# Moving the sums of the second weights between VectorE and GpSimd in a fused attention and feed-forward kernel

## The chip, the cores and the metric

One core of a Trainium2 chip. The time is that of one execution on the device in microseconds, the median of several runs; lower is better.

## What is computed

Attention within chunks of 64 rows, over 8 heads of 64 features, and then a layer norm with a gain `g`, a feed-forward net of 512 to 2048 to 512 features with a ReLU between, and a sum with its input. There are 8 x 576 = 4608 rows, and all data are float32 (the arrays arrive as given below; the kernel's weights are handed over as 64-bit words).

```
def _attn_ref(q, k, v):                       # 8, 8, 576, 64; chunks of 64 rows
    scores = scale * q_c @ k_c.transpose(0, 1, 2, 4, 3)
    scores = scores - max(scores); attn = exp(scores)
    attn = attn / (sum(attn) + 1e-09)
    return attn @ v_c
def _moe_ref(x, g_ln, w_ch1, w_ch2):          # x: 8, 576, 512
    xn = (x - mu) / sqrt(var + 1e-06) * g_ln
    return x + max(xn @ w_ch1, 0.0) @ w_ch2
```

## The kernel before

**Tiles and units.** The rows form 18 pairs of 256 rows, and two pairs make a tile. The first three tiles go through the net in the plain way. The other six make two units of two pairs of pairs each, whose products are done by a scheme with seven products in place of eight (Strassen's in Winograd's form). For that the weights are needed as seven sums and differences of their blocks. Each float32 product is made of three passes: a rounded high part and the rest, called `hh` and `hl` (or `his` and what is left) in the code.

**The sums of the weights.** `prepare` (stream S, on GpSimd) makes those of the first weights during the second tile and the start of the third, and writes them to `wa` in DRAM. `mix` makes those of the second weights during the third tile: for each of eight parts p (weights 2p and 2p + 1), two sums of the high and the low half (L975, 128x512), four sums and differences of blocks (L982, 128x256), a rounded copy by ScalarE (L985), two subtractions that give the rest (L988, 128x512), and the writes to `wb` in DRAM (L992, L993). Each part does that in eight steps. Streams a, b, c are parts 1, 2, 3 on VectorE; T is parts 4 and 5 on GpSimd, V part 6 on GpSimd, W part 7 on VectorE; d is part 0, read back from DRAM, on VectorE.

**The order by hand.** All engines work off their own queues in the order in which the program issues to them. That order is written down: `THIRD` gives, for each of 32 tokens of the third tile's net, which streams take one step each before the token. A token `u1` is a first product of the net (twelve matmuls, L560) and its split into `hh` (ScalarE, L573) and `hl` (VectorE, L574); a token `u` is a second product (twelve matmuls, L584). C, G, D and H are the attentions of the pairs of the first unit: G1 loads q and k, G2 is the scores (L304), G3 their maxima (VectorE, L311), G4 the difference (VectorE, L336), G5 the exponent (ScalarE), G6 to G9 the transposes by VectorE (L375), G10 the sums, G11 the product with v (L404), G12 its scaling. D9 is a scaling (L430), D10 the statistics (L448 to L454, the last of them `rstd` on GpSimd), D11 the centring (VectorE, L460), D12 the scaling by `rstd` (ScalarE), D13 and D14 the transposes by TensorE (L492) and their copies. P and Q (`combine`) make the first unit's operands from the rows: casts on ScalarE (L781), differences on VectorE (L788), subtractions on GpSimd (L785).

**Places.** PSUM has two banks named `s` (one buffer, for scores, transposes and some products), two named `h` (for the first products, and for G11, which takes both) and four named `y`. A tile of SBUF with the tag `w5`, say, takes the place of weight 5 when that is no longer read. A new tile in a place waits for all readers of the old one.

**The units.** `unit_ffn` runs the seven products (L1031), four groups of fourteen, with sums on VectorE into `hu` (L1040) and copies on ScalarE into `snap` (L1037), and then the second products (L943). Weights come through a ring of six places of 512 KB. `weave` lets other streams take steps at given costs, where each product of six matmuls costs 6.

Of the kernel before, what the change touches and what calls it, by code (L numbers as in the profile page):

```python
# [8 lines left out]
F32 = mybir.dt.float32  # L9
# [32 lines left out]
    23: "BCS", 24: "BCS", 25: "CS", 26: "S", 27: "CCS", 28: "CS", 29: "CCS", 30: "CDS", 31: "CDDS", 32: "DS",  # L42
}
THIRD = {
    0: "CS", 1: "CS", 2: "DDGS", 3: "DS", 4: "DDS", 5: "DS", 6: "DGSaa", 7: "GGHSTTaa", 8: "DGTTabb", 9: "Daaabb",
    10: "GGPTcc", 11: "HGGPTTbcc", 12: "GTTTbb", 13: "GTTbc", 14: "GGHPcc", 15: "GHPTc", 16: "GHPTT", 17: "GPTVV",
    18: "HHGPVV", 19: "HGP", 20: "HGPV", 21: "HHPVVd", 22: "HPV", 23: "WW", 24: "HWW", 25: "Hdd", 26: "QQWdd",
    27: "QRWW", 28: "QWd", 29: "QXXNdd", 30: "QQRd", 31: "Q",
}
ROOMS = {1: (3, 9), 2: (6,)}  # L50

# [4 lines left out]
AT_END = (0, 6, 11, 18, 33, 37, 40, 48, 54, 82, 92, 97, 104, 109, 121, 133, 146)  # L56
PAIR_STEPS = (STEPS, BY_TENSOR, WIDE, AT_END)
HALVES = ((512, 8), (612, 10))
REST = (2, 6, 20)


# [41 lines left out]
def chunk_attention_ffn(ctx: ExitStack, tc: tile.TileContext, qkv, v01, g, w, out):  # L103
# [31 lines left out]
    def weights(f):  # L135
        if f not in wp:
            wp[f] = const.tile([P, 2, NW], F32R, name="wp", tag=f"w{f}")
        return wp[f][:, 0, :], wp[f][:, 1, :]
# [514 lines left out]
    def bring(pairs):  # L653
        for pair in pairs:
            back[pair] = unspill(pair)
            yield
# [312 lines left out]
                    yield 3.17  # L969
                    self.advance(t + (k + 1) / 2)  # L970

    def mix(p, t_, his, parts_of, engine):
        for k in range(2):
            high, low = parts_of(k)
            engine.tensor_tensor(out=t_[:, k], in0=high, in1=low, op=ALU.add)  # L975
            yield
        b11, b12, b21, b22 = (t_[:, k // 2, k % 2 * PAIR : (k % 2 + 1) * PAIR] for k in range(4))
        for k, (out, x, y, op) in enumerate((
            (b11, b12, b11, ALU.subtract), (b12, b22, b12, ALU.subtract), (b22, b11, b22, ALU.subtract),
            (b21, b21, b22, ALU.add),  # L980
        )):
            engine.tensor_tensor(out=out, in0=x, in1=y, op=op)  # L982
            if k % 2:
                yield
        nc.scalar.copy(his, t_)  # L985
        yield
        for k in range(2):
            engine.tensor_tensor(  # L988
                out=t_[:, k].bitcast(F32R), in0=t_[:, k], in1=his[:, k].bitcast(F32), op=ALU.subtract
            )  # L990
            yield
        nc.sync.dma_start(wb[:, p, 0], his.rearrange("p f (a n) -> p (f a) n", a=2).bitcast(F32))  # L992
        nc.sync.dma_start(wb[:, p, 1], t_.rearrange("p f (a n) -> p (f a) n", a=2))  # L993
        yield

    def mix_early(pool, tag, ps, engine):
        for p in ps:
            t_ = pool.tile([P, 2, 2, DM], F32, name="mixed", tag=tag)
            yield from mix(
                p, t_[:, 0], t_[:, 1].bitcast(F32R),  # L1000
                lambda k: [x[:, DM:].bitcast(F32) for x in weights(2 * p + k)], engine,
            )

    def mix_again(tag, p):
        t_ = const.tile([P, 2, 2, DM], F32, name="mixed", tag=tag)
        for k in range(2):
            nc.sync.dma_start(t_[:, :, k], w2d[2 * p + k])
        yield
        yield from mix(
            p, t_[:, 0], t_[:, 1].bitcast(F32R), lambda k: [t_[:, 0, k], t_[:, 1, k]], nc.vector  # L1010
        )

    def unit_ffn(u):
        first = 2 * LEAD + 4 * u
        hu = {}
        for n in range(2):
            for f in range(NF):
                if f // 2 not in hu:
                    hu[f // 2] = shared.setdefault(
                        f"h{f // 2}", None  # L1020
                    ) or const.tile([P, 2, 2, DM], F32, name="hu", tag=f"w{8 + f // 2}")
                    shared[f"h{f // 2}"] = hu[f // 2]
        snaps = [raws.tile([P, n, DM], F32, name="snap", tag=g) for n, g in ((4, "raw"), (2, "wf"))]
        snaps = [x[:, i] for x in snaps for i in range(x.shape[1])]

# [39 lines left out]
        for q in range(NF // 4):  # L1065
            banks = [ps_y.tile([P, DM], F32, name="y") for _ in range(4)]
            c_, a_ = banks[0::2], banks[1::2]
            h = [hu[2 * q], hu[2 * q + 1]]
            s = [snaps[:3], snaps[3:]]

            def pair_of():
                w = ring.take()[:, : 2 * DM].rearrange("p (i h n) -> p i h n", i=2, h=2)
                return w[:, 0], w[:, 1]

            steps = []
            for e in range(2):
                steps += [
                    (c_, e, "2", None),
                    (a_, e, "1", lambda e: (copy(s[e][0], a_[e]), add(h[e][:, 0, 0], c_[e], s[e][0]))),
                ]  # L1080
            for e in range(2):
                steps += [
                    (a_, e, "6", lambda e: copy(s[e][1], a_[e])),
                    (c_, e, "5", lambda e: copy(s[e][2], c_[e])),
                ]
            for e in range(2):
                steps += [
                    (a_, e, "7", lambda e: add(h[e][:, 1, 1], a_[e], s[e][2])),
                    (c_, e, "3", lambda e: add(h[e][:, 1, 0], c_[e], s[e][1])),
                ]  # L1090
            for e in range(2):
                steps += [
                    (a_, e, "4", lambda e: nc.scalar.activation(h[e][:, 0, 1], a_[e], AF.Relu))
                ]
            for i, (bank, e, name, then) in enumerate(steps):
                if i % 2 == 0:
                    w01 = pair_of()
                product(bank[e], w01[i % 2], name, name in "215")
                yield 6
                if i % 2:  # L1100
                    ring.fetch()
                if then:
                    then(e)
                if name == "7":
                    waiting.append((14 * q + i + 2, h[e][:, 1, 1]))
                if waiting and waiting[0][0] <= 14 * q + i:
                    relu(waiting.pop(0)[1])
                if q > 0 and i in (4, 6):
                    mix_1(2 * (q - 1) + i // 2 - 2)
                if q == NF // 4 - 1:  # L1110
                    plan.advance((i + 1 - len(steps)) * 0.945)
                    if i in (12, 13):
                        mix_1(2 * q + i - 12)
# [48 lines left out]
    with tc.manual_schedule():  # L1162
        nc.scalar.activation(minus, ident, AF.Copy, scale=-1.0)
        play(START, now)
        now.update(
            A=now.pop("E"), B=tiles[2].attention(1), C=tiles[3].attention(0, True), D=tiles[4].attention(0, True),
            G=tiles[3].attention(1), H=tiles[4].attention(1, True, pt_raw=True), S=prepare(), R=start_ring(), T=mix_early(raws, "raw", (4, 5), nc.gpsimd),
            V=mix_early(const, "w7", (6,), nc.gpsimd), W=mix_early(const, "w8", (7,), nc.vector), X=bring(range(2 * LEAD - 2, 2 * LEAD)),
            a=mix_early(const, "w1", (1,), nc.vector), b=mix_early(const, "w2", (2,), nc.vector), c=mix_early(const, "w3", (3,), nc.vector),
            d=mix_again("w9", 0), P=combine(0, 0), Q=combine(0, 1),  # L1170
        )
        now.update(zip("u1", tiles[1].ffn(0, 2, room=ROOMS[1])))
        play(layout(ROOMS[1], SECOND), now)
        streams = {}

        def following(u, n):
            n, u = n % 4, u + n // 4
            if (u, n) not in streams and u < UNITS:
                by_pe = len(PAIR_STEPS[n]) == len(BY_TENSOR)
                streams[u, n] = tiles[LEAD + 2 * u + n % 2].attention(n // 2, pt_by_pe=by_pe)  # L1180
            return streams.get((u, n), iter(" "))

        now["N"] = following(1, 0)
        now.update(zip("u1", tiles[2].ffn(0, 2, room=ROOMS[2])))
        play(layout(ROOMS[2], THIRD, True), now)
        side = [(at, now["Q"]) for at in REST]
        for u in range(UNITS):
            if u + 1 < UNITS:
                for n in range(4):
                    begin, steps = BEGINS[n], PAIR_STEPS[n]  # L1190
                    side += [(begin + at, following(u + 1, n)) for at in steps]
                    side.append((begin + steps[0], following(u + 1, n + 1)))
                for half, (begin, step) in enumerate(HALVES):
                    stream = combine(u + 1, half)
                    side += [(begin + i * step, stream) for i in range(13)]
            side = weave(unit_ffn(u), side)
        assert not side
# [35 lines left out]
```

## Time and profile before

| | us |
|---|---|
| median of 3 runs | 839.59 (837.94 to 843.39) |
| the profiled execution | 839.96 |
| its span, first to last instruction | 838.0 |
| TensorE busy | 818.5 (98%) |
| VectorE busy | 643.5 (77%) |
| ScalarE busy | 345.8 (41%) |
| GpSimd busy | 179.3 (21%) |

The third tile's net runs from about 228 to 338 us of the span. A row of the timeline gives the start, the busy time, the engine, the line, the operation, what it writes and reads, its size and count, and in brackets the engine's idle time before it with what ended it. PE is TensorE, DVE VectorE, ACT ScalarE, POOL GpSimd; a q behind a name means the engine's queue. A row of stretches gives the limits, the length, the busy time and count of PE, PEld (weight loads), DVE, ACT and POOL, and then the granted TensorE clock, the share of the DMA engines and GB/s.

### The profile page before, as it was taken

To read this page: it belongs to the slowest core of one execution; us is meant where nothing else is said; L and a number is where in the kernel's file an instruction comes from. 1 tells how busy PE (TensorE), PEld (TensorE's weight loads), DVE (VectorE), ACT (ScalarE), POOL (GpSimd) and SP (SyncE) were. 2 spreads that over 40 slices of the span, in tenths; PEclk is the share of its full clock that TensorE was granted. 3 is DMA by queue.
4 is the path that set the end of the run, shared out by engine and by line. 5 is a ranking of instruction groups with operands and counts; after the bars stand their busy time and mean duration, and the time that the engine had idled before them with its cause. 6 is when DMAs were issued, how large, how long until landed. Compare 5 with 4: busy or idle time off the path is not lost.

```text
span 838.0 us, 16961 instructions
## 1 busy us (share of the span) xinstructions
PE 818.5 (98%) x6746; PEld 713.6 (85%) x6746; DVE 643.5 (77%) x1023; ACT 345.8 (41%) x545; POOL 179.3 (21%) x148
## 2 busy tenths in 40 slices
PE   7999999999998799999999999999999999999998
PEld 4888888888887587888899998788999988889998
DVE  6989966777659998779788998898889953248854
ACT  4776431122333234243364453434555632255432
POOL 0111006463855374100000270000002700000000
PEclk9999999999999799999999999999999999999999
DMA  9998417948884435978889659788796686668662
GB/s 357 334 267 237 157 45 240 327 163 289 306 287 160 192 126 214 398 258 265 286 251 305 212 177 352 236 275 253 226 303 218 182 295 190 190 198 278 212 214 101
DMA packets 117278, 200.62 MB, mean 239 GB/s; under 512 B 8784, under 2 KB 75856, under 8 KB 115280
## 3 DMA queue, kind: packets, MB, share of 16 engines
q1 hardware_dynamic: 115904, 194.82, 68.7%
q0 software_dynamic: 1296, 4.72, 2.9%
q8 instruction: 53, 0.87, 0.4%
q14 instruction: 25, 0.20, 0.1%
HBM read 141.84 MB, written 48.76 MB: 227 GB/s over the span
## 4 chain that ended last, share of the span: by engine, by line
PE 89%; DVE 7%; DMA 2%; ACT 1%; issue 1%; SPq 0%; DVEq 0%; ACTq 0%
PE y L943 29%; PE y L1031 26%; PE y L584 14%; PE h L560 14%; PE s L304 2%; DVE pt_sb L375 2%; PE h L404 1%; DVE mixed L982 1%; DMA wp<-wfs 1%; DMA k_t<-qkv 1%; PE s L404 1%; PE s L330 0%; PE s L363 0%; PE s L353 0%; DVE mixed L975 0%
## 5 line engine op out<-in xcount | busy, mean ns | idle before, releaser
L1031 PE MATMUL y<-xc,ring 128*128 128x512 f32 x1008 | 235.2, 392 | 0.2 <-DVE hu L1040 0.2
L1031 PEld LDWEIGHTS y<-xc,ring 128*128 128x128 f32 x1008 | 187.5, 188 | 39.8 <-DVE hu L1040 0.6
L943 PE MATMUL y<-ring,hx 128*128 128x256 f32 x1272 | 158.0, 283 | 0.0
L943 PEld LDWEIGHTS y<-ring,hx 128*128 128x128 f32 x1272 | 155.0, 192 | 0.0
L560 PE MATMUL h<-xth,wp 128*128 128x512 f32 (+1 forms) x432 | 129.5, 370 | 0.9 <-DMA wp<-wfs 0.9
L1040 DVE TENSOR_TENSOR hu<-y,snap 128x512 f32<-128x512 f32 x72 | 49.2, 686 | 69.0 <-PE y L1031 34.7
L584 PE MATMUL y<-wp,hh 128*128 128x512 f32 x376 | 97.9, 399 | 0.0
L880 ACT ACTIVATE hx<-hu 128x512 fp32r<-128x512 f32 x106 | 65.8, 630 | 65.8 <-PE y L943 60.9
L560 PEld LDWEIGHTS h<-xth,wp 128*128 128x128 f32 x432 | 78.2, 188 | 15.4 <-DMA wp<-wfs 1.1
L785 POOL TENSOR_TENSOR xc<-rows,xc 128x512 fp32r<-128x512 f32 x28 | 60.5, 2173 | 128.8 <-ACT xc L781 127.2
L584 PEld LDWEIGHTS y<-wp,hh 128*128 128x128 f32 x376 | 70.1, 191 | 14.3
L889 DVE TENSOR_TENSOR hx<-hu,hx 128x512 fp32r<-128x512 f32 x90 | 67.4, 758 | 15.1 <-ACT hx L880 13.2
L560 PE MATMUL h<-xtl,wp 128*128 128x512 f32 (+1 forms) x216 | 78.3, 367 | 0.0
L573 ACT ACTIVATE hh<-h 128x512 fp32r<-128x512 f32 (+1 forms) x53 | 28.5, 545 | 109.0 <-PE h L560 109.0
L1037 ACT COPY snap<-y 128x512 f32<-128x512 f32 x72 | 41.7, 585 | 73.4 <-PE y L1031 73.4
L943 PE MATMUL y<-ring,hh 128*128 128x256 f32 x496 | 71.8, 283 | 0.0
L574 DVE SCALAR_TENSOR_TENSOR hl<-h,hh 128x512 fp32r<-128x512 f32 (+1 forms) x53 | 32.9, 627 | 45.8 <-ACT hh L573 45.4
L943 PEld LDWEIGHTS y<-ring,hh 128*128 128x128 f32 x496 | 65.2, 192 | 0.2
L584 PE MATMUL y<-wp,hl 128*128 128x512 f32 x188 | 51.9, 390 | 0.0
L880 ACT ACTIVATE hh<-hu 128x512 fp32r<-128x512 f32 x62 | 38.8, 631 | 31.6 <-PE y L943 29.1
L375 DVE STREAM_TRANSPOSE pt_sb<-p_sb 32x256 f32<-32x256 f32 x112 | 48.8, 436 | 3.6 <-ACT p_sb L339 1.7
L454 POOL TENSOR_TENSOR rstd<-vare,mhalf 128x2 f32<-128x2 f32 x12 | 10.0, 831 | 190.2 <-DVE vare L453 190.2
(146 smaller groups left out, 1084.4 us busy)
## 6 DMA issues: line engine op xcount, KB each, us to landing
ring<-wa SPq DMA_DIRECT2D x84, 512.0 KB, 4.6
ring<-wb SPq DMA_DIRECT2D x48, 512.0 KB, 3.8
ring<-w2d SPq DMA_DIRECT2D x36, 512.0 KB, 3.8
raw<-w SPq DMA_DIRECT2D x15, 1024.0 KB, 7.7
out<-x SPq DMA_DIRECT2D x22, 512.0 KB, 5.4
q_t<-qkv SPq DMA_DIRECT2D x17, 512.0 KB, 6.1
k_t<-qkv SPq DMA_DIRECT2D x17, 512.0 KB, 7.0
v_t<-qkv SPq DMA_DIRECT2D x32, 256.0 KB, 7.1
```

The lines of the kernel that those rows point to most:

```text
L375: nc.vector.transpose(out=pt_sb[quad(2 * h2 + j), :, c, quad(i)], in_=p_sb[quad(2 * c + i), :, h2, quad(j)])
L560: nc.tensor.matmul(h, lhsT=(wh, wh, wl)[m][:, ks], rhs=(xth, xtl, xth)[m][:, k, :], start=i == 0, stop=i == len(terms) - 1,)
L573: nc.scalar.activation(hh, h, AF.Relu)
L574: nc.vector.scalar_tensor_tensor(out=hl, in0=h, scalar=0.0, in1=hh.bitcast(F32), op0=ALU.max, op1=ALU.subtract)
L584: nc.tensor.matmul(sums(pairs[j // 2])[j % 2], lhsT=(hh, hh, hl)[m], rhs=(wh, wl, wh)[m], start=f == 0 and m == 0, stop=f == NF - 1 and m ...
L785: engine.tensor_tensor(out=o[:, 1], in0=x, in1=o[:, 0].bitcast(F32), op=ALU.subtract)
L880: nc.scalar.activation(hh, self.split[i][2], AF.Relu if x == "1" else AF.Copy)
L889: nc.vector.tensor_tensor(out=hl, in0=x, in1=hh.bitcast(F32), op=ALU.subtract)
L943: nc.tensor.matmul(bank[j // 2][:, j % 2 * PAIR : (j % 2 + 1) * PAIR], lhsT=(hh, hh, hl)[m][:, j * P : (j + 1) * P], rhs=loaded[t // 2][:, ...
L1031: nc.tensor.matmul(bank, lhsT=w[:, (0, 0, 1)[m], ks], rhs=x[:, (0, 1, 0)[m], k, :], start=start and k == m == 0, stop=k == 1 and m == 2, s ...
L1037: nc.scalar.copy(out, bank)
L1040: nc.vector.tensor_tensor(out=out, in0=bank, in1=s, op=ALU.add)
```

## The change

Part 2 (stream b) goes from VectorE to GpSimd. Part 7 leaves the third tile: a stream of its own on GpSimd makes it in the first unit, at the costs `MIX_STEPS`, in the place of weight 13. Part 5 has a stream of its own (U), beside T for part 4. Parts 1, 2, 3 are put into the places of weights 0, 1, 2 and not 1, 2, 3, and part 1 begins at token 4 and not 6, part 2 at token 6 and not 8, part 3 at token 9 and not 10. Within several tokens the steps of a, c and d now come ahead of the attention's steps. `mix` makes the rounded copy in two halves and writes `wb` in four pieces of 256 KB and not two of 512 KB. The places of `hu` are handed out group by group.

```
 THIRD = {
-    0: "CS", 1: "CS", 2: "DDGS", 3: "DS", 4: "DDS", 5: "DS", 6: "DGSaa", 7: "GGHSTTaa", 8: "DGTTabb", 9: "Daaabb",
-    10: "GGPTcc", 11: "HGGPTTbcc", 12: "GTTTbb", 13: "GTTbc", 14: "GGHPcc", 15: "GHPTc", 16: "GHPTT", 17: "GPTVV",
-    18: "HHGPVV", 19: "HGP", 20: "HGPV", 21: "HHPVVd", 22: "HPV", 23: "WW", 24: "HWW", 25: "Hdd", 26: "QQWdd",
-    27: "QRWW", 28: "QWd", 29: "QXXNdd", 30: "QQRd", 31: "Q",
+    0: "CS", 1: "CS", 2: "DDGS", 3: "DS", 4: "aaDDS", 5: "aaDS", 6: "aDGSbb", 7: "aaGGHSbbTT", 8: "aDGTT", 9: "ccDb",
+    10: "ccGGPbbbT", 11: "HGGTT", 12: "cGTUU", 13: "GPUU", 14: "GGHP", 15: "ccGHPU", 16: "cGHPUU", 17: "GPUVV",
+    18: "HHGPVV", 19: "HGP", 20: "HGPV", 21: "HHPVVd", 22: "HPV", 24: "H", 25: "ddH", 26: "ddQQ", 27: "QR", 28: "dQ",
+    29: "ddQXXN", 30: "dQQR", 31: "Q",
 }
+MIX_STEPS = (24, 26, 30, 34, 54, 60, 62, 76)

-    def mix(p, t_, his, parts_of, engine):
+    def mix(p, engine, pool, tag, again=False):
+        both = pool.tile([P, 2, 2, DM], F32, name="mixed", tag=tag)
+        t_, his = ([both[:, i, k] for k in range(2)] for i in range(2))
...
-        nc.scalar.copy(his, t_)
-        yield
         for k in range(2):
-            engine.tensor_tensor(
-                out=t_[:, k].bitcast(F32R), in0=t_[:, k], in1=his[:, k].bitcast(F32), op=ALU.subtract
-            )
-            yield
-        nc.sync.dma_start(wb[:, p, 0], his.rearrange("p f (a n) -> p (f a) n", a=2).bitcast(F32))
-        nc.sync.dma_start(wb[:, p, 1], t_.rearrange("p f (a n) -> p (f a) n", a=2))
-        yield
+            nc.scalar.copy(his[k].bitcast(F32R), t_[k])
+        yield
+        for k in range(2):
+            engine.tensor_tensor(out=t_[k].bitcast(F32R), in0=t_[k], in1=his[k], op=ALU.subtract)
+            yield
+        for k in range(2):
+            for h, x in enumerate((his, t_)):
+                nc.sync.dma_start(wb[:, p, h, 2 * k : 2 * k + 2], x[k].rearrange("p (a n) -> p a n", a=2))
+        yield
...
+            for p in (2 * q, 2 * q + 1):
+                name = f"h{p}"
+                if name not in shared:
+                    shared[name] = const.tile([P, 2, 2, DM], F32, name="hu", tag=f"w{8 + p}")
+                hu[p] = shared[name]
...
-            G=tiles[3].attention(1), H=tiles[4].attention(1, True, pt_raw=True), S=prepare(), R=start_ring(), T=mix_early(raws, "raw", (4, 5), nc.gpsimd),
-            V=mix_early(const, "w7", (6,), nc.gpsimd), W=mix_early(const, "w8", (7,), nc.vector), X=bring(range(2 * LEAD - 2, 2 * LEAD)),
-            a=mix_early(const, "w1", (1,), nc.vector), b=mix_early(const, "w2", (2,), nc.vector), c=mix_early(const, "w3", (3,), nc.vector),
-            d=mix_again("w9", 0), P=combine(0, 0), Q=combine(0, 1),
+            G=tiles[3].attention(1), H=tiles[4].attention(1, True, pt_raw=True), S=prepare(), R=start_ring(), T=mix(4, nc.gpsimd, raws, "raw"),
+            U=mix(5, nc.gpsimd, raws, "raw"), V=mix(6, nc.gpsimd, const, "w7"), a=mix(1, nc.vector, const, "w0"),
+            b=mix(2, nc.gpsimd, const, "w1"), c=mix(3, nc.vector, const, "w2"), d=mix(0, nc.vector, const, "w9", True),
+            X=bring(range(2 * LEAD - 2, 2 * LEAD)), P=combine(0, 0), Q=combine(0, 1),
...
         side = [(at, now["Q"]) for at in REST]
+        stream = mix(NF // 2 - 1, nc.gpsimd, const, "w13")
+        side += [(at, stream) for at in MIX_STEPS]
```

More of the change, by code (lines that the diff above doesn't have):

```diff
@@ L970, in products @@
                     self.advance(t + (k + 1) / 2)
-    def mix(p, t_, his, parts_of, engine):
+    def mix(p, engine, pool, tag, again=False):
+        both = pool.tile([P, 2, 2, DM], F32, name="mixed", tag=tag)
+        t_, his = ([both[:, i, k] for k in range(2)] for i in range(2))
+        if again:
+            blocks = [[t_[k], his[k]] for k in range(2)]
+            for k in range(2):
+                nc.sync.dma_start(both[:, :, k], w2d[2 * p + k])
+            yield
+        else:
+            blocks = [[x[:, DM:].bitcast(F32) for x in weights(2 * p + k)] for k in range(2)]
         for k in range(2):
-            high, low = parts_of(k)
-            engine.tensor_tensor(out=t_[:, k], in0=high, in1=low, op=ALU.add)
+            engine.tensor_tensor(out=t_[k], in0=blocks[k][0], in1=blocks[k][1], op=ALU.add)
             yield
-        b11, b12, b21, b22 = (t_[:, k // 2, k % 2 * PAIR : (k % 2 + 1) * PAIR] for k in range(4))
+        b11, b12, b21, b22 = (t_[k // 2][:, k % 2 * PAIR : (k % 2 + 1) * PAIR] for k in range(4))
         for k, (out, x, y, op) in enumerate((
@@ L984, in mix @@
                 yield
-        nc.scalar.copy(his, t_)
+        for k in range(2):
+            nc.scalar.copy(his[k].bitcast(F32R), t_[k])
         yield
         for k in range(2):
-            engine.tensor_tensor(
-                out=t_[:, k].bitcast(F32R), in0=t_[:, k], in1=his[:, k].bitcast(F32), op=ALU.subtract
-            )
+            engine.tensor_tensor(out=t_[k].bitcast(F32R), in0=t_[k], in1=his[k], op=ALU.subtract)
             yield
-        nc.sync.dma_start(wb[:, p, 0], his.rearrange("p f (a n) -> p (f a) n", a=2).bitcast(F32))
-        nc.sync.dma_start(wb[:, p, 1], t_.rearrange("p f (a n) -> p (f a) n", a=2))
+        for k in range(2):
+            for h, x in enumerate((his, t_)):
+                nc.sync.dma_start(wb[:, p, h, 2 * k : 2 * k + 2], x[k].rearrange("p (a n) -> p a n", a=2))
         yield
[L996 to L1007, printed above, removed]
-        yield
-        yield from mix(
-            p, t_[:, 0], t_[:, 1].bitcast(F32R), lambda k: [t_[:, 0, k], t_[:, 1, k]], nc.vector
-        )
     def unit_ffn(u):
@@ L1015, in unit_ffn @@
         hu = {}
[L1016 to L1022, printed above, removed]
         snaps = [raws.tile([P, n, DM], F32, name="snap", tag=g) for n, g in ((4, "raw"), (2, "wf"))]
```

## The prediction

> **What bounds the kernel now.** I read the engine totals first, then the chain of waits in order of time, then the timelines of TensorE, VectorE and GpSimd where that chain leaves TensorE.
>
> ```profile
> PE 818.5 (98%) x6746; PEld 713.6 (85%) x6746; DVE 643.5 (77%) x1023; ACT 345.8 (41%) x545; POOL 179.3 (21%) x148
> ```
>
> TensorE is busy for 818.5 of 838.0 us, so little can be won: only where it stands still, or runs slowly, inside the third tile. These are its rows there.
>
> ```profile
> 253.85 0.60 PE L492 MATMUL s<-ident,xg 128*128 128x128 f32 x4
> ...
> 260.27 1.98 PE L584 MATMUL y<-wp,hh 128*128 128x512 f32 x8
> ...
> 269.85 0.33 PE L404 MATMUL h<-v_t,pt_sb 64*64 64x64 f32 x4
> 278.30 1.97 PE L404 MATMUL h<-v_t,pt_sb 64*64 64x64 f32 x60 [8.12 <-DVE hl L574]
> ...
> 333.04 1.22 PE L584 MATMUL y<-wp,last 128*128 128x512 f32 x3 [0.70 <-ACT last L573]
> ```
>
> The products of G's attention (L404) get through four matmuls and then stand for 8.12 us, until VectorE's `hl` frees the second `h` bank. At the tile's end 0.70 us are lost to ScalarE. The chain after the first stop, and the granted clock around it:
>
> ```profile
> 280.27 4.65 PE y L584 x12
> 284.92 5.45 PE h L560 x24
> 290.38 2.72 PE y L584 x12
> 274.00:278.00 4.00, 0.00 (x0) 0.00 (x0) 3.92 (x4) 0.32 (x1) 3.92 (x4) 0.50 0.09 37
> 278.00:282.00 4.00, 3.70 (x64) 3.27 (x65) 3.93 (x8) 0.72 (x1) 1.69 (x3) 0.50 0.00 0
> 282.00:286.00 4.00, 4.00 (x15) 3.15 (x14) 3.86 (x8) 0.00 (x0) 0.70 (x1) 0.76 0.96 336
> ```
>
> TensorE comes back at half clock (0.50; in these rows it is the third figure from the right): twelve matmuls of L584 take 4.65 us and not 2.72, a loss of 1.93, and of the 1.97 us of sixty L404 half is lost, so the clock costs 1.93 + 0.98 = 2.9 us. All that the third tile can give back is 8.12 + 2.9 + 0.70 = 11.7 us, 1.4%. Why VectorE is late stands in its own rows:
>
> ```profile
> 246.14 1.41 DVE L460 SCALAR_TENSOR_TENSOR xg<-x,mv,g_sb 128x512 f32<-128x512 f32 x2
> 247.91 0.69 DVE L574 SCALAR_TENSOR_TENSOR hl<-h,hh 128x512 fp32r<-128x512 f32 x1 [0.36 <-ACT hh L573]
> 248.52 2.44 DVE L975 TENSOR_TENSOR mixed<-wp 128x512 f32<-128x512 f32 x2
> 250.88 1.21 DVE L311 TENSOR_REDUCE top<-s 128x16 f32<-128x1024 f32 x1
> 252.12 1.22 DVE L336 TENSOR_TENSOR p_sb<-s,top 128x1024 f32<-128x1024 f32 x1
> 253.27 1.79 DVE L982 TENSOR_TENSOR mixed<-mixed 128x256 f32<-128x256 f32 x4
> 254.98 0.68 DVE L574 SCALAR_TENSOR_TENSOR hl<-h,hh 128x512 fp32r<-128x512 f32 x1
> 255.58 1.28 DVE L975 TENSOR_TENSOR mixed<-wp 128x512 f32<-128x512 f32 x2
> 257.11 1.29 DVE L988 TENSOR_TENSOR mixed<-mixed 128x512 fp32r<-128x512 f32 x2 [0.25 <-ACT mixed L985]
> 258.32 4.16 DVE L982 TENSOR_TENSOR mixed<-mixed 128x256 f32<-128x256 f32 x4
> 262.40 0.68 DVE L574 SCALAR_TENSOR_TENSOR hl<-h,hh 128x512 fp32r<-128x512 f32 x1
> 263.00 3.58 DVE L375 STREAM_TRANSPOSE pt_sb<-p_sb 32x256 f32<-32x256 f32 x8
> 266.61 3.30 DVE L975 TENSOR_TENSOR mixed<-wp 128x512 f32<-128x512 f32 x2
> 269.93 3.60 DVE L375 STREAM_TRANSPOSE pt_sb<-p_sb 32x256 f32<-32x256 f32 x8
> 273.56 4.09 DVE L982 TENSOR_TENSOR mixed<-mixed 128x256 f32<-128x256 f32 x4
> 277.57 0.68 DVE L574 SCALAR_TENSOR_TENSOR hl<-h,hh 128x512 fp32r<-128x512 f32 x1
> 246.31 1.13 POOL L454 TENSOR_TENSOR rstd<-vare,mhalf 128x2 f32<-128x2 f32 x1 [6.81 <-DVE vare L453]
> 247.42 2.38 POOL L692 TENSOR_TENSOR parts<-sums,parts 128x1024 fp32r<-128x1024 f32 x1
> 258.43 2.88 POOL L975 TENSOR_TENSOR mixed<-wp 128x512 f32<-128x512 f32 x2 [8.63 <-DMA wa<-parts]
> ```
>
> VectorE never rests from 248 to 278 us. The same operation has two prices: two sums of L975 take 1.28 us with GpSimd idle and 2.44 while GpSimd's L692 runs; four steps of L982 take 1.79 alone and 4.16 beside GpSimd's L975. Operations that read PSUM (L311, L336, L574) and the transposes keep their time. So two-input operations of VectorE on SBUF wait for a GpSimd operation to end. The Trainium skill, "SBUF — State Buffer", section "SBUF: two separate sides", calls this an exclusive lock between the two engines, held for a whole instruction. By it, work moved to GpSimd can come back to VectorE as waiting, which speaks against this change; without it the sum would be that of the first rival below. The trace agrees (2.44 for 1.28, 4.16 for 1.79).
>
> **The change, part by part.** *Ahead of D13.* D13, the transposes at L492, writes the `s` banks, of which there is one set; it must wait until L336 of G (G4) has read them. Before, L336 ends at 253.34 and TensorE, straight from product 4, comes at 253.85: 0.5 us of slack. After, part 1 (`a`) starts in token 4 and all of its VectorE work stands before L336. Uncontended, it adds two sums (255.58 to 256.86, 1.20 in sequence), four steps (253.27 to 254.98, 1.71) and two subtractions (257.11 to 258.32, 1.21). It takes out the old sums (248.52 to 250.88, 2.36) and the idle 0.36 us at 247.91. That is +1.40: L336 ends at 254.74, and D13 stands for about 1.0 us. This is the lower end.
>
> GpSimd comes on top. The first sums delay L430 and the statistics by 1.20, so `rstd` and then L692 start 1.20 later: L692 runs from 248.62 to 251.0. VectorE is then at its third L982 of part 1; the fourth, and both L460, have two inputs in SBUF.
>
> ```profile
> 158.93 1.89 DVE L460 SCALAR_TENSOR_TENSOR xg<-x,mv,g_sb 128x512 f32<-128x512 f32 x2
> ```
>
> That pair, beside GpSimd's sums in the second tile, took 1.89 and not 1.41: L460 waits too. So the fourth step ends at about 251.3. Now GpSimd begins part 2 (`b`, new there): its two sums, 1.4 us each as in the row at 258.43. The two L460 alternate with them, 2 x 1.4, to 254.1; L574, 0.6, to 254.7; the two subtractions beside GpSimd's four steps cost 1.9 like the row above, to 256.6; L311 and L336 another 2.4: 259.0. **D13 stands for 5.1 us** (bounds 1.0 and 6). L574 at 254.7 holds nobody up: its product comes behind D13.
>
> *From there to G's products.* All that follows TensorE shifts by 5.1: product 5's first half, which ended at 260.27, ends at 265.4.
>
> ```profile
> 260.53 0.60 ACT L573 ACTIVATE hh<-h 128x512 fp32r<-128x512 f32 x1 [2.25 <-PE h L560]
> ...
> 331.87 0.62 ACT L781 CAST xc<-rows 128x512 fp32r<-128x512 f32 x1 [3.50 <-DVE rows L788]
> 332.40 0.59 ACT L573 ACTIVATE last<-h 128x512 fp32r<-128x512 f32 x1
> ```
>
> ScalarE's `hh` then ends at 266.25 (0.26 + 0.60), VectorE's `hl` at 266.85. Part 3's sums are done before, in VectorE's wait for it. Behind it stand part 3's four steps (1.71 alone, 4.09 in the row at 273.56); GpSimd then has P1's subtraction and part 2's two, so I take one free step and three at 1.4: 4.6. Then the transposes, 3.6 + 3.6, and `hl`, 0.6: 279.3. TensorE is there at 270.18 + 5.1 = 275.3 and **stands again for 4.0 us**. L404 resumes at 279.3, not 278.30: **+1.0** (from -5.9, with 1.0 and 1.7 in place of 5.1 and 4.6, to +2.5). Part 2 is gone from VectorE's queue (1.28 + 4.16 + 1.2 = 6.6 us), and the gain goes into waiting for GpSimd and, once TensorE is late, for `hh`.
>
> *The clock.* Idle 0.70 us left it alone; idle 8.12 us halved it. Stops of 5.1 and 4.0 lie between: from no drop (-2.9) to two (+2.9). I take one, the same as before: **0**. The Trainium skill, "TensorE: Matmul & The Clock Gate", section "What's actually happening", names a free-running window of about 3.4 us that must pass idle; by it alone the stops, as an estimate, would drop it with chances of about a half and a sixth, or 0.7 drops, some 0.9 us less. The rows at 274 and 282 fit it.
>
> *The tile's end.* Part 7 (`W`) leaves tokens 23 to 28. ScalarE's `last` stood behind a cast that waited for VectorE's rows (331.87). With 4 to 7 us fewer on VectorE that row is ready earlier: **-0.7**, not more, since TensorE has no other gap there.
>
> *Part 7 in the first unit.* Its steps on GpSimd lie four to thirteen products into the unit; the row is from that stretch.
>
> ```profile
> 346.00:350.00 4.00, 4.00 (x20) 3.30 (x19) 3.81 (x9) 2.65 (x5) 1.29 (x1) 1.00 1.03 405
> ```
>
> GpSimd has 1.29 us of 4 to do there and ScalarE 2.65; VectorE is full (3.81), but with transposes and with sums that read PSUM, which keep their time beside GpSimd: 0. Without that cover, ScalarE's two casts (0.62 each, as at 331.87) would stand before the `snap` copies that free TensorE's banks, some 1.2 us. The 1 MB of its result leaves while the DMA share is about 1, with six ring places in hand: 0. The later handing out of the `hu` places costs nothing: part 7's place goes to the third of four groups, long after. Each part's casts are two of half the size, on an engine busy for 41%: 0. `wb` is written in four pieces and not two, the bytes being the same, by a queue that waits for VectorE anyway. SP meets part 1's writes behind G's and H's loads, so it holds no load up. ScalarE's cast in P1 now needs part 1's place (`w0`) written out: the writes are issued at about 257, the cast comes at 266: 0.
>
> **Sum:** +1.0 + 0 - 0.7 = +0.3 us on a span of 838.0, whose execution took 839.96. The median is 0.37 lower: 839.59 + 0.3 = 839.9.
>
> **Rivals.** *VectorE is freed as meant.* If GpSimd's operations slip between VectorE's, D13 stands 1.0 us and L404 resumes at 272.4: -5.9 - 2.9 (no stop is long) - 0.7 = -9.5, 830. For it: 6.6 us less work in a queue that is the bound; against it: 2.44 and 4.16. Half of the contention gives about 834. *No clock drop*: +0.3 - 2.9 gives 837; it needs both stops to fall short. *Slower: the one stop becomes two, each with its own clock drop.* Place: D13 and L404; price +0.3 + 2.9 = +3.2, 843; with part 2 wholly in the way (+2.5 in place of +1.0) 844.5. It decides when both stops are long enough for the clock to fall; the one known drop came within 4 us of TensorE's stop at 270.2.
>
> **How the numbers follow.** Forecast 839.9: 0.45; no drop, 837: 0.2; freed wholly or half, 830 to 835: 0.2; two drops, 843 to 844.5: 0.15. The range 833 to 844.5 leaves out most of the freed case. 1% (8.4 us) is what a measurement of this kernel can tell from no change; faster than 831.2 needs nearly all of the 11.7 us: 0.10. Slower than 848 needs more than two drops: 0.04.
>
> **What would show it.** Right: a gap before L492 near 254 us that ends with VectorE's L336; L460 and part 1's subtractions stretched beside GpSimd; a second gap before L404, shorter than 8.12; the 0.70 gap gone; no gap in the first unit. Wrong: L492 at 253.9 with no gap (contention over-counted), or a first unit whose products wait for GpSimd's `mixed`.

## The result, and the profile after

The changed kernel is slower: 845.58 us (843.47 to 846.85) against 839.59, ratio 1.007 (95% interval 1.0044 to 1.0096). Run once more beside other kernels it took 844.58 against 838.98, ratio 1.0055 (1.0034 to 1.0076). The prediction said no change, 839.9, and its range ended at 844.5.

The profiled execution took 843.47, its span is 841.7 us, 3.7 more than before. Lines have moved: L304 to L943 of before are one higher, L975, L982 and L988 are L984, L991 and L998, and L1031 and L1040 are L1016 and L1025. TensorE's timeline of the changed kernel, in the third tile:

```profile
259.04 1.09 PE L493 MATMUL s<-ident,xg 128*128 128x128 f32 x4 [5.50 <-DVE p_sb L337]
...
277.78 0.33 PE L405 MATMUL h<-v_t,pt_sb 64*64 64x64 f32 x2 [0.29 <-DVE pt_sb L376]
278.70 0.33 PE L405 MATMUL h<-v_t,pt_sb 64*64 64x64 f32 x2 [0.59 <-DVE pt_sb L376]
283.04 1.97 PE L405 MATMUL h<-v_t,pt_sb 64*64 64x64 f32 x60 [4.02 <-DVE hl L575]
```

One stop of 8.12 us has become two: 5.50 us before D13's transposes, which wait for VectorE's L337 to leave the `s` banks, and 0.29 + 0.59 + 4.02 = 4.9 us at G's products. The 0.70 us at the tile's end is gone. The chain of waits after each stop, and the stretches with the granted clock (the third figure from the right):

```profile
260.13 4.67 PE y L585 x12
264.80 0.44 PE s L493 x4
265.23 2.79 PE h L561 x12
...
283.04 1.97 PE h L405 x60
285.01 4.37 PE y L585 x12
```

```profile
257.00:261.00 4.00, 1.96 (x7) 1.80 (x8) 3.96 (x5) 0.83 (x2) 3.92 (x5) 0.54 0.36 135
261.00:265.00 4.00, 4.00 (x15) 3.13 (x14) 1.02 (x1) 0.71 (x1) 2.99 (x4) 0.61 0.00 0
...
277.00:281.00 4.00, 1.14 (x7) 0.44 (x5) 3.84 (x10) 0.00 (x0) 2.35 (x2) 1.00 0.27 103
281.00:285.00 4.00, 1.96 (x61) 1.84 (x61) 3.84 (x7) 0.00 (x0) 3.77 (x6) 0.52 0.00 0
```

Both stops halved the clock, where the kernel before paid for that once: twelve L585 take 4.67 and 4.37 us and not 2.72. VectorE's timeline shows who is late, GpSimd's why:

```profile
242.01 0.69 DVE L575 SCALAR_TENSOR_TENSOR hl<-h,hh 128x512 fp32r<-128x512 f32 x1 [5.07 <-ACT hh L574]
...
246.89 3.87 DVE L991 TENSOR_TENSOR mixed<-mixed 128x256 f32<-128x256 f32 x4
250.69 3.49 DVE L461 SCALAR_TENSOR_TENSOR xg<-x,mv,g_sb 128x512 f32<-128x512 f32 x2
254.09 0.68 DVE L575 SCALAR_TENSOR_TENSOR hl<-h,hh 128x512 fp32r<-128x512 f32 x1
254.69 1.80 DVE L998 TENSOR_TENSOR mixed<-mixed 128x512 fp32r<-128x512 f32 x2
256.42 1.21 DVE L312 TENSOR_REDUCE top<-s 128x16 f32<-128x1024 f32 x1
257.67 1.22 DVE L337 TENSOR_TENSOR p_sb<-s,top 128x1024 f32<-128x1024 f32 x1
...
268.73 0.69 DVE L575 SCALAR_TENSOR_TENSOR hl<-h,hh 128x512 fp32r<-128x512 f32 x1 [6.71 <-ACT hh L574]
269.34 5.80 DVE L991 TENSOR_TENSOR mixed<-mixed 128x256 f32<-128x256 f32 x4
275.06 7.21 DVE L376 STREAM_TRANSPOSE pt_sb<-p_sb 32x256 f32<-32x256 f32 x16
282.30 0.69 DVE L575 SCALAR_TENSOR_TENSOR hl<-h,hh 128x512 fp32r<-128x512 f32 x1
```

```profile
247.84 2.64 POOL L693 TENSOR_TENSOR parts<-sums,parts 128x1024 fp32r<-128x1024 f32 x1
250.44 3.18 POOL L984 TENSOR_TENSOR mixed<-wp 128x512 f32<-128x512 f32 x2
253.59 4.29 POOL L991 TENSOR_TENSOR mixed<-mixed 128x256 f32<-128x256 f32 x4
...
269.28 1.29 POOL L786 TENSOR_TENSOR xc<-rows,xc 128x512 fp32r<-128x512 f32 x1 [5.06 <-ACT xc L782]
270.53 5.76 POOL L998 TENSOR_TENSOR mixed<-mixed 128x512 fp32r<-128x512 f32 x4
```

Part 1's four steps end behind GpSimd's L693, the two L461 take 3.49 us beside part 2's sums where they took 1.41, and L337 ends at 258.89. Then VectorE idles 6.71 us for ScalarE's `hh`, because TensorE is late, and only then do part 3's steps come, 5.80 us beside GpSimd's L786 and L998.

### The profile page after: what moved, and what is told of

Its sections match the earlier page's. It is cut to its first block, busy times and chain, and to the rows that moved or that the text cites. A ratio compares the mean times of both kernels' runs of the same rounds, so it can differ in the third digit from the quotient of the medians.

```text
span 841.7 us, 17010 instructions
## 1 busy us (share of the span) xinstructions
PE 821.6 (98%) x6746; PEld 715.5 (85%) x6746; DVE 635.9 (76%) x1007; ACT 347.2 (41%) x553; POOL 195.1 (23%) x164
## 4 chain that ended last, share of the span: by engine, by line
PE 86%; DVE 8%; DMA 2%; POOL 1%; SPq 1%; ACT 1%; issue 0%; DVEq 0%; POOLq 0%; ACTq 0%
PE y L944 29%; PE y L1016 26%; PE y L585 13%; PE h L561 13%; PE s L305 2%; DVE pt_sb L376 2%; PE h L405 1%; DVE mixed L991 1%; DMA wp<-wfs 1%; DMA k_t<-qkv 1%; DVE xg L461 1%; DMA wa<-wp 1%; DVE hl L575 0%; PE s L405 0%; PE s L331 0%
## 5 line engine op out<-in xcount | busy, mean ns | idle before, releaser
L1016 PE MATMUL y<-xc,ring 128*128 128x512 f32 x1008 | 235.1, 392 | 0.2 <-DVE hu L1025 0.2
L1016 PEld LDWEIGHTS y<-xc,ring 128*128 128x128 f32 x1008 | 187.5, 188 | 39.8 <-DVE hu L1025 0.6
L1025 DVE TENSOR_TENSOR hu<-y,snap 128x512 f32<-128x512 f32 x72 | 49.2, 686 | 69.0 <-PE y L1016 34.7
L585 PE MATMUL y<-wp,hh 128*128 128x512 f32 x376 | 99.3, 404 | 0.0
L786 POOL TENSOR_TENSOR xc<-rows,xc 128x512 fp32r<-128x512 f32 x28 | 60.1, 2158 | 135.3 <-ACT xc L782 133.7
L585 PEld LDWEIGHTS y<-wp,hh 128*128 128x128 f32 x376 | 71.3, 194 | 14.6
L585 PE MATMUL y<-wp,hl 128*128 128x512 f32 x188 | 52.2, 392 | 0.0
```

The lines of the kernel that those rows point to most:

```text
L585: nc.tensor.matmul(sums(pairs[j // 2])[j % 2], lhsT=(hh, hh, hl)[m], rhs=(wh, wl, wh)[m], start=f == 0 and m == 0, stop=f == NF - 1 and m ...
L786: engine.tensor_tensor(out=o[:, 1], in0=x, in1=o[:, 0].bitcast(F32), op=ALU.subtract)
L1016: nc.tensor.matmul(bank, lhsT=w[:, (0, 0, 1)[m], ks], rhs=x[:, (0, 1, 0)[m], k, :], start=start and k == m == 0, stop=k == 1 and m == 2, s ...
L1025: nc.vector.tensor_tensor(out=out, in0=bank, in1=s, op=ALU.add)
```

## The experiments

All were timed against the kernel before on the same chip. Theory S is the prediction's mechanism with one step changed after the result: D13 stands behind the `s` banks and G's products stand again, as predicted, and each long stop halves the clock, where the prediction took one drop in all. Its rivals are named in the expectations: that VectorE's time beside GpSimd is the price wherever the attention's steps stand (L), and that part 7's new place costs (U).

**G3 and G4 first.**

```
-    ... 7: "aaGGHSbbTT",
+    ... 7: "GGaaHSbbTT",
```

> Changed kernel with G3 and G4 ahead of part 1's subtractions in token 7. Theory S (TensorE's D13 stands because VectorE reads the `s` banks late; each long stop also halves the clock): L336 ends some 1.7 us sooner, the stop before L493 shrinks from 5.5 to about 3.8 us, the time from 845.6 to 843 or 844. Rival L (what costs is the VectorE time lost beside GpSimd, wherever the attention's steps stand): the stop before L405 grows by what the first one loses, 845.6.

Measured: 841.99 us against 839.77, ratio 1.0029 (1.0013 to 1.0045). Its TensorE timeline, its chain and its stretches:

```profile
257.61 0.63 PE L493 MATMUL s<-ident,xg 128*128 128x128 f32 x4 [3.76 <-DVE p_sb L337]
...
279.24 1.97 PE L405 MATMUL h<-v_t,pt_sb 64*64 64x64 f32 x60 [4.03 <-DVE hl L575]
```

```profile
258.24 2.74 PE y L585 x12
260.98 0.44 PE s L493 x4
261.42 2.79 PE h L561 x12
```

```profile
255.00:259.00 4.00, 1.39 (x8) 1.25 (x9) 3.97 (x5) 1.44 (x4) 3.77 (x5) 1.00 0.33 123
259.00:263.00 4.00, 4.00 (x21) 3.32 (x20) 3.61 (x4) 2.37 (x4) 3.92 (x4) 1.00 0.51 194
```

The stop is 3.76 us, as S said, and the one before L405 stays at 4.03 us, where L would have it grow; L's time of 845.6 lies outside too. In the profiled execution this stop did not halve the clock, and that prices the first drop: from the start of L493 to the end of the next first product the changed kernel needs 268.02 - 259.04 = 8.98 us, this one 264.21 - 257.61 = 6.60. A drop costs 2.4 us.

That execution was the fastest of the twelve, though, at 839.02 us and a mean granted clock of 0.995. The other eleven show 0.991 to 0.994, and 3.41 us at half clock take 0.002 off the mean of such a span. So in most of them this stop probably did halve the clock for a while, and why the median lies 1 us below S's 843 is not shown.

**Part 2 later.**

```
-    ... 6: "aDGSbb", 7: "aaGGHSbbTT", 8: "aDGTT", 9: "ccDb",
-    10: "ccGGPbbbT", 11: "HGGTT", 12: "cGTUU", ...
+    ... 6: "aDGS", 7: "aaGGHSTT", 8: "aDGTTbb", 9: "ccDbb",
+    10: "ccGGPT", 11: "HGGTTbbb", 12: "cGTbUU", ...
```

> Changed kernel with part 2 on GpSimd two tokens later (tokens 8 to 12 in place of 6 to 10). Theory S with the waits beside GpSimd as their main price: both L461 and part 1's subtractions meet only L693, the stop before L493 is about 3.0 us and not 5.5, and one clock drop may go: 841 to 843. If the place of part 1 ahead of G3 is the price and not GpSimd: stop of 5 us or more, 845 to 846.

Measured: 838.22 us against 839.77, ratio 0.9977 (0.9962 to 0.9992). TensorE, VectorE, and one stretch of it:

```profile
259.72 0.63 PE L493 MATMUL s<-ident,xg 128*128 128x128 f32 x4 [2.88 <-DVE p_sb L337]
280.21 1.19 PE L405 MATMUL h<-v_t,pt_sb 64*64 64x64 f32 x60 [2.56 <-DVE hl L575]
```

```profile
250.19 3.87 DVE L991 TENSOR_TENSOR mixed<-mixed 128x256 f32<-128x256 f32 x4
253.98 1.40 DVE L461 SCALAR_TENSOR_TENSOR xg<-x,mv,g_sb 128x512 f32<-128x512 f32 x2
255.30 0.68 DVE L575 SCALAR_TENSOR_TENSOR hl<-h,hh 128x512 fp32r<-128x512 f32 x1
255.90 1.28 DVE L998 TENSOR_TENSOR mixed<-mixed 128x512 fp32r<-128x512 f32 x2
```

```profile
261.00:265.00 4.00, 4.00 (x15) 3.16 (x14) 0.37 (x1) 0.93 (x1) 3.92 (x4) 0.61 0.06 24
```

VectorE's order is the changed kernel's; only GpSimd is empty beside it, apart from L693, which still holds the four steps at 3.87. L461 is back at 1.40 (from 3.49) and the subtractions at 1.28 (from 1.80). The stop is 2.88 us for an expected 3.0. So 2.6 of the 5.50 us are the waits for part 2 on GpSimd, and the rest is part 1's place ahead of G3 and the wait for L693. The time fell further than expected, since the stop before L405 fell as well, to 2.56: part 3's steps met less of GpSimd too and took 3.06 us and not 5.80. No drop went; each of the two stops was followed by 3.41 us at half clock, where the changed kernel has 6.83 us for each of its stops.

**Part 7 alone moved.**

```
-    ... 23: "WW", 24: "HWW", 25: "Hdd", 26: "QQWdd", 27: "QRWW", 28: "QWd",
-            ... W=mix_early(const, "w8", (7,), nc.vector), ...
+    ... 24: "H", 25: "Hdd", 26: "QQdd", 27: "QR", 28: "Qd",
+        stream = mix_early(const, "w13", (7,), nc.gpsimd)
+        side += [(at, stream) for at in MIX_STEPS]
```

> The kernel before with part 7 alone moved to GpSimd in the first unit (and the `hu` places handed out group by group). Theory S: the 0.70 us gap at the tile's end goes, nothing is lost in the unit: 838.9 against 839.6 of before. Rival U (part 7 in the unit or its writes cost what the prediction missed): 842 or more, with a gap in the first unit.

Measured: 839.09 us against 839.77, ratio 0.9987 (0.9973 to 1.0002). TensorE's only stop in the tile is the old one:

```profile
278.60 1.97 PE L405 MATMUL h<-v_t,pt_sb 64*64 64x64 f32 x60 [7.87 <-DVE hl L575]
```

The 0.70 us gap is gone and U's 842 lies outside; the gain of 0.7 us itself is within the interval. In the changed kernel itself, two stretches of the first unit that hold part 7 show TensorE full and GpSimd at work:

```profile
350.00:354.00 4.00, 4.00 (x19) 3.30 (x19) 3.84 (x9) 2.36 (x5) 3.70 (x3) 1.00 1.03 388
354.00:358.00 4.00, 4.00 (x20) 3.30 (x19) 3.82 (x9) 1.93 (x4) 3.77 (x6) 1.00 0.57 186
```

The six tiles behind the third make three units, not two as the description of the kernel has it. From the first product of the first unit (338.38 us before, 342.10 after) to the start of the last row of second products (753.56 and 757.23) both kernels need the same, 415.2 and 415.1 us. So all that the profiled execution of the changed kernel lost, it lost before the first unit.

**D13 later.**

```
-    ... 8: "aDGTT", 9: "ccDb", 10: "ccGGPbbbT", 11: "HGGTT", 12: "cGTUU", ...
+    ... 8: "aGTT", 9: "ccb", 10: "DccGGPbbbT", 11: "DGGTT", 12: "HcGTUU", ...
```

> Changed kernel with TensorE's D13 and D14 two tokens later (tokens 10 and 11) and H2 at 12, so that two more products stand before the transposes. Theory S: no stop before L493 and no clock drop there; part 3's steps then start some 8 us sooner, L405 resumes at about 275 and not 283 us, one stop of about 5 us with one drop stays: 836 to 838. Rival L: VectorE's queue is as late as ever, the whole stop moves to L405: 844 to 846.

Measured: 835.22 us against 839.77, ratio 0.995 (0.9933 to 0.9966), a little faster than S had it. The stop before L493 is 0.07 us, and one is left:

```profile
274.01 1.98 PE L405 MATMUL h<-v_t,pt_sb 64*64 64x64 f32 x60 [4.02 <-DVE hl L575]
```

VectorE's and GpSimd's queues kept their order; TensorE only does two more products before it asks for the `s` banks. That alone takes 9 to 10 us from the changed kernel (845.58 to 835.22, or 844.58 in its second session). L, by which the stop would only move to L405, is out.

**Part 2 alone on GpSimd, in the kernel before.**

```
-            ... b=mix_early(const, "w2", (2,), nc.vector), ...
+            ... b=mix_early(const, "w2", (2,), nc.gpsimd), ...
```

> The kernel before with part 2 alone on GpSimd, all places in the order as before (G3 and G4 ahead of part 1). Theory S: no stop before L492; part 2's 6.6 us leave VectorE's queue, part 3's steps come beside more of GpSimd's work; L404 resumes at about 277 and not 278.3 us; 837 to 839. Rival L (GpSimd's part 2 costs VectorE more than it gives): 841 or more.

Measured: 838.95 us against 838.98, ratio 0.9999 (0.9985 to 1.0014).

```profile
277.92 1.97 PE L404 MATMUL h<-v_t,pt_sb 64*64 64x64 f32 x60 [7.06 <-DVE hl L574]
```

The stop shrank by 1.1 us (8.12 to 7.06) and no new one came, but the time doesn't show it: taking 6.6 us from VectorE's queue shortens the stop by a sixth of that. VectorE's rows show where the rest went, into waits for ScalarE and into part 3's steps beside more of GpSimd (5.09 us and not 4.09):

```profile
257.79 1.29 DVE L988 TENSOR_TENSOR mixed<-mixed 128x512 fp32r<-128x512 f32 x2 [1.45 <-ACT mixed L985]
261.85 0.69 DVE L574 SCALAR_TENSOR_TENSOR hl<-h,hh 128x512 fp32r<-128x512 f32 x1 [2.77 <-ACT hh L573]
...
272.17 5.09 DVE L982 TENSOR_TENSOR mixed<-mixed 128x256 f32<-128x256 f32 x4
```

So moving part 2 to GpSimd is not by itself what made the change slow. It hurt in the changed kernel, where it stood beside part 1 ahead of G3: with part 2 two tokens later that kernel took 838.22 us.

**Part 1 back behind G3 and G4, part 2 on GpSimd.**

```
-    ... 4: "aaDDS", 5: "aaDS", 6: "aDGSbb", 7: "aaGGHSbbTT", 8: "aDGTT", 9: "ccDb",
-    10: "ccGGPbbbT", 11: "HGGTT", ...
+    ... 4: "DDS", 5: "DS", 6: "DGSaabb", 7: "GGHSaabbTT", 8: "aDGTT", 9: "aaaccDb",
+    10: "ccGGbbbT", 11: "HGGPTT", ...
```

> Changed kernel with part 1 put back behind G3 and G4 (tokens 6 to 9, as before; P1 one token later), part 2 still on GpSimd. Theory S: no stop before L493; one stop before L405 of 4 to 5 us with one clock drop; 835 to 838. Rival L: the stop before L405 grows to 8 us or more, 841 to 846.

Measured: 835.73 us against 838.98, ratio 0.9959 (0.9943 to 0.9975).

```profile
254.92 0.63 PE L493 MATMUL s<-ident,xg 128*128 128x128 f32 x4 [0.60 <-DVE p_sb L337]
...
275.30 1.98 PE L405 MATMUL h<-v_t,pt_sb 64*64 64x64 f32 x60 [3.45 <-DVE hl L575]
```

With part 1's place undone the 5.50 us fall to 0.60, and the kernel is faster than before. So it is the place of part 1 that opened the first stop, from VectorE's side as D13's places did from TensorE's; part 2, at the same tokens as in the changed kernel, costs no such stop without it. This kernel also keeps the other parts of the change (the halved copies, the four writes, the new places of weights and `hu`, part 7 in the unit), so none of them made it slow.

**Part 3 later as well.** The kernel with D13 later, and part 3 behind G12 and G13.

```
-    ... 10: "DccGGPbbbT", 11: "DGGTT", 12: "HcGTUU", 13: "GPUU", 14: "GGHP", 15: "ccGHPU", 16: "cGHPUU", 17: "GPUVV",
+    ... 10: "DGGPbbbT", 11: "DGGTT", 12: "HGTUU", 13: "GPUU", 14: "GGHPcc", 15: "cGHPU", 16: "ccGHPUU", 17: "cGPUVV",
-            ... c=mix(3, nc.vector, const, "w2"), ...
+            ... c=mix(3, nc.vector, const, "w3"), ...
```

> The kernel with D13, D14 and H2 later, and part 3's steps besides moved behind G12 and G13 (its differences in token 14, its subtractions in token 16, place of weight 3). Theory S: nothing of the mixing stands before VectorE's transposes for L405 any more, so its stop of 4.0 us falls under 1 us, no clock drop is left: 829 to 831. Rival L: VectorE then misses the scaling or H's exponent, and a stop of several us comes before the products after L405: 834 or more.

Measured: 830.62 us against 838.98, ratio 0.9894 (0.9872 to 0.9916).

```profile
271.11 1.15 PE L405 MATMUL h<-v_t,pt_sb 64*64 64x64 f32 x60 [0.95 <-DVE hl L575]
282.80 1.20 PE L585 MATMUL y<-wp,hl 128*128 128x512 f32 x4 [0.33 <-DVE hl L575]
```

Both long stops are gone, and TensorE comes back at full speed: sixty L405 take 1.15 us and not 1.97. (So the clock had cost them 0.8 us, and not half of the 1.97 as the prediction took it.) This version beats the kernel before by 8.4 us, and the prediction's 11.7 us had named what was there to be had.

**The changed kernel again.**

> The changed kernel unchanged, beside the others of this call. Theory S (D13 stands behind the `s` banks, G's products stand again, and each stop halves the clock): two stops of about 5.5 and 4.9 us and two stretches at half clock again, 844 to 846. If the second clock drop was a chance of the one profile: one drop, 842 to 843.

Measured: 844.58 us, as given at the top. Its profile shows stops of 5.49 and 4.92 us in the same places, each followed by a stretch at half clock. The second drop was no chance of one execution.

## Why the prediction was wrong, point by point

**D13 behind the `s` banks: right.** 5.1 us were predicted, 5.50 measured, and the two experiments that undo it from either side take it to 0.07 and 0.60. The waits beside GpSimd were right one by one: the fourth step behind L693, the L461 one for one with part 2's sums. The place of part 1 and GpSimd's part 2 beside it are both in the prediction's sum.

**The second stop: right in kind.** 4.0 us predicted, 4.9 measured. But sixty L405 start 4.7 us later than in the kernel before and not 1.0, beyond the text's own upper bound of +2.5, for which it gives no working; the next two points are what it lacked. **The tile's end and part 7 in the first unit: right**, as the rows of both stretches and the third experiment show. The lone move of part 2 leaves the time where it was, and its gain does go into waiting, as stated.

**The clock: the step that failed.** The text had two bounds, none and two drops, and took one, "the same as before: 0". There were two: the stops of 5.50 and 4.9 us each brought 6.83 us at half clock. The first of them, worth 2.4 us, is also in series with everything after it: product 5's first half ends at 268.02 and not 265.4, so `hh`, part 3's steps and G's transposes are all later by that.

**Part 3's steps: mis-sized.** 4.6 us were taken, one free step and three at 1.4. It was 5.80: none was free, because GpSimd was inside L786 or L998, each of 512 elements, the whole time: one L786 and four L998, the last two of them part 4's, where the prediction counted three operations in all. The row of before that served as the upper bound (4.09) ended beside shorter GpSimd operations of 256 elements, so it was no bound.

With these two, the sum of the profiled execution closes. It ran 0.46 us ahead at the start of this part, with `hl` at 242.01 where the kernel before has it at 242.47:

```profile
242.47 0.69 DVE L574 SCALAR_TENSOR_TENSOR hl<-h,hh 128x512 fp32r<-128x512 f32 x1 [5.08 <-ACT hh L573]
```

To the predicted +0.3 come 0.5 for D13 (259.04 + 0.46 and not 259.0), 2.4 for the first drop, 1.0 for part 3's steps (269.42 to 275.06 is 5.6) and -0.3 for the second drop, which cost less than the old one (283.04 to 289.38 against 278.30 to 284.92): +3.9. Less 0.46 that is 3.4, for 3.7 of the spans. The medians differ by 6.0 and 5.6; the profiled execution was the fastest of its seven runs, and what the others spent more was not traced, so some 2 us of the 6 stay open. More drops are not the whole of it: executions at the same granted clock of 0.991 took from 843.47 to 845.72 us.

**The rival on the slower side** had the mechanism as it came, one stop becoming two with a clock drop each, at 843 to 844.5 and a chance of 0.15. By the text's own figures it deserved more weight: both stops came out at 4 us or more, and the one known drop came 3.5 us after TensorE's stop (270.2 to 273.6). The Trainium skill ("TensorE: Matmul & The Clock Gate", section "What's actually happening"), read as asking for a window that passes wholly idle, had spoken for fewer drops. The experiments don't bear that reading out: a stop of 2.88 us was followed by one.

## What to carry to other kernels

When an engine is late, list each place where another engine takes over a single-buffered resource behind it, and see which of them the reordering makes late: here 6.6 us off a queue bought nothing that the time shows, while the consumer's place, two products later, was worth 9 us. In these traces work given to GpSimd is paid for on VectorE by the two-input operations on SBUF that stand beside it, at about the length of the GpSimd operation; put it beside transposes or operations that read PSUM. And count the stops as well as their length: here each long one brought its own stretch at half clock, and the first cost 2.4 us on top of its 5.50.

## What the runs showed of the hardware

In these traces the third tile's stretches at half clock last 3.41, 6.83 or 10.24 us, and within one trace the changes of the clock lie whole multiples of 3.41 us apart: in the changed kernel it falls at 257.29, rises at 264.12, falls at 281.18 and rises at 288.01. A stop need not be that long to bring a drop. In the kernel with part 2 later, a stop of 2.88 us was followed by half clock (0.61 in the stretch from 261 to 265 us), and so was its stop of 2.56 us, while with G3 and G4 first a stop of 3.76 us left it at 1.00. The length of the stop alone does not decide.

Where the stop falls among steps of 3.41 us, counted from the changes of the clock, explains part of it: the stop of 2.88 us has 2.4 us in one step, that of 3.76 us at most 1.9 in any. But with part 1 back the stop of 3.45 us has only 1.8 us in the step that ends with the drop, so what decides stays open. The stops of 5.50, 4.9, 7.06, 7.87 and 8.12 us were all followed by a drop, and so were those of 4.02 and 3.45 us: their sixty L405 took 1.98 us, where 1.15 to 1.19 is the time at full clock.

A VectorE step of 0.43 us beside GpSimd operations of about 1.4 us took 1.4 to 1.5 us, one for one, and GpSimd's own operations stretched as well: four L991 of part 2 took 4.29 us beside VectorE's L461 and L998, and 3.58 with G3 and G4 first, where VectorE's L312 and L337, which read PSUM, stood in the place of L998.
